# Attention's query products held still in TensorE, with x brought to its partitions by DMAs

## The chip, the cores and the metric

The kernel runs on one core of one Trainium2 chip. The metric is device time in microseconds of one execution; the median of three runs of the kernel before is 496.31 us (496.24 to 496.53). All data is float32.

## The reference

Two blocks follow each other. The first is attention with a polynomial feature map, for 4 batches, 4 heads, 1,088 tokens and head dimension 32. The second is a sum of four two-layer experts over the 4,352 tokens, weighted by gates. Cut to what matters:

```python
def phi(x):                       # 8 x 8 = 64 features of a token
    a = np.einsum('rd,bhsd->bhsr', S1, x)
    b = np.einsum('rd,bhsd->bhsr', S2, x)
    return np.einsum('bhsi,bhsj->bhsij', a, b).reshape(*x.shape[:-1], 64)
q_p, k_p = phi(q), phi(k)
kv = np.einsum('bhsf,bhsd->bhfd', k_p, v)
z = np.sum(k_p, axis=2)
num = np.einsum('bhsf,bhfd->bhsd', q_p, kv)
den = np.einsum('bhsf,bhf->bhs', q_p, z)[..., None] + 1e-06
attn = num / den
x = attn.transpose(0, 2, 1, 3).reshape(4352, 128)      # (token, head x dim)
p = domain_probs / (domain_probs.sum(-1, keepdims=True) + 1e-09)
for e in range(4):
    out += p[:, e:e + 1] * (np.maximum(x @ w1[e], 0) @ w2[e])    # 128 -> 1024 -> 128
```

## The kernel before

The order of all work is written out by hand. A batch's tokens are cut into units (`UNITS`: 128, 480, 480 in batch 0, then 384, 352, 352), for which attention is computed, and all tokens into eleven chunks (`CHUNKS`: 128, 480, 480, five of 512, 320, 256, 128), for which the experts are computed. A chunk has 16 steps, one for each pair of 128-wide blocks of the hidden layer of an expert. The main loop at the end of the program (from line 766) runs over all steps of all chunks; `first` (L573) of a step computes h = x @ w1 and the rectified values and their sums, and `second` (L623), two steps later (`LA`), multiplies them with w2. In the chunks between the first and the last, the second product uses sums of blocks of weights (seven products of 64 x 64 blocks for eight). TensorE works in two halves of 64 output columns each; `on_side` (L184) sends matmuls to the halves in turn, `both` (L190) one to each, and all of them carry the line L188.

Attention is cut into pieces (`front`, L547): a batch's keys are 17 pieces, a unit's queries 19. `work()`, called twice in each step, executes as many pieces as a credit allows. The credit grows by `rate`, so that a chunk's pieces are done 4 pieces before the chunk begins (`needed[c] + 4`); where they are not, they are executed ahead of the chunk's first step. A piece's instructions stand in its engine's order just where it is executed, so an engine does a piece between the instructions of two steps.

For a unit of n tokens, `queries` (L452) turns q in 32 x 32 blocks (`query_turn`, L403), projects it with S1 and S2 on TensorE (`f<-qT,sq`), and makes the feature products `qp` on VectorE (L412; two tiles of 128 features, two heads each). Then `attend` (L419) multiplies: the keys' sums kv, and their divisors z repeated 32 times, both laid out by `key_divide` (L370) in blocks for two heads (`kvz`), stand still in TensorE, and the n columns of `qp` move. The results `den` and `num` have (head, dim) on the partitions and tokens along the free dimension. VectorE turns den, takes reciprocals of one value of 32, turns them back (`rb`) and multiplies num into `xT` (L446). This is the layout that `first` reads as its moving operand: x with its 128 features on the partitions.

The first unit, and the keys of batch 0, are done in `start` (L497) before any chunk. All DMAs are issued on the sync engine's queue (SPq), in program order[...]. They are the loads of k, v and q of a batch (`load_batch`), of the weights, of a chunk's gates, broadcast to 128 partitions (`load_gate`, L299; two buffers), and the stores of a chunk's output (L694, L653).

`weight_sums` on GpSimd is held back until `behind` (L788), a copy of one column of x of unit (0, 128).

Of the kernel before, what the change touches and what calls it, by code (L numbers as in the profile page):

```python
# [23 lines left out]
def kernel(  # L24
# [25 lines left out]
    P = 128  # L50
# [7 lines left out]
    NT = 9  # L58
    FB = F // P
    NQ = E * FB // 2  # L60
    QW = 480
    CW = 512
    GE = 160
    LA = 2
    UNITS = [[P, 480, 480]] + [[384, 352, 352]] * 3

    CHUNKS = [P, 480, 480] + [512] * 5 + [320, 256, P]
    NC = len(CHUNKS)
    START = [sum(CHUNKS[:m]) for m in range(NC)]
    assert all(sum(u) == S for u in UNITS) and sum(CHUNKS) == B * S  # L70
# [12 lines left out]
    def psum(pool, tag):  # L83
        return pool.tile([P, 512], F32, tag=tag, name=tag)
# [27 lines left out]
    def load_batch(b):  # L112
        load_rows(k, b, "kn")
        vn[b] = load_v(b)
        load_rows(q, b, "qn")
# [29 lines left out]
    e_sum = cpool.tile([P, 2, 3], F32, name="e_sum")  # L145
    for i, t in enumerate((0, (B - 1) * S + G - 4)):
        nc.sync.dma_start(
            ends[:, i, :], bass.AP(domain_probs.tensor, domain_probs.offset + t * E, [[E, 4], [G * E, 32], [1, E]])
        )
    load_rows(q, 0, "qn", slice(P, S))  # L150
    for e in range(E):
# [20 lines left out]
    def keep_warm(n):  # L172

        for _ in range(n):
            wp = psum(ps_h, "h")
            nc.tensor.matmul(wp[:, :], warm[:, 0:P], warm[:, :], start=True, stop=True)  # L176

    keep_warm(11)


    turn = [0]
# [123 lines left out]


    FG = ((0, 4), (4, 4), (8, 1))
    fss, kps, kvzs = {}, {}, {}

    def key_turn(b, r):  # L310
        if r < 2:
# [58 lines left out]
    def key_divide(b, kv):  # L370
# [8 lines left out]
            )  # L379
        kvzs[b] = kvz  # L380

    def keys(b):
        for r in range(3):
            key_turn(b, r)
            yield
        for gi, (pool, tag) in enumerate(((ps_f, "f"), (ps_n, "den"), (ps_n, "num"))):
            key_project(b, gi, psum(pool, tag))
            yield
        for _ in value_copy(b):
            pass  # L390
        for t0, n in ((0, 4), (4, 5)):
            for p in range(2):
                for x in range(2):
                    key_product(b, t0, n, p, x, nc.vector)
                    yield
        kv = psum(ps_f, "f")
        for p in range(2):
            key_sum(b, p, kv)
            yield
        key_divide(b, kv)  # L400
        yield

    def query_turn(b, c, n):  # L403
        qT = apool.tile([P, QW], F32, tag="qT", name="qT")
        nc.vector.transpose(qT[:, 0:n], qn[b][:, c : c + n])
        return qT

    def query_tiles():
# [7 lines left out]
            op=ALU.mult,  # L416
        )

    def attend(b, c, n, qp):  # L419
# [12 lines left out]
        yield  # L432
        dT = apool.tile([P, QW], F32, tag="dT", name="dT")
# [7 lines left out]
        rb = apool.tile([P, QW], F32, tag="rb", name="rb")  # L441
# [4 lines left out]
        nc.vector.tensor_tensor(  # L446
            out=xT[:, S * b + c : S * b + c + n], in0=nd[1][:, 0:n], in1=rb[:, 0:n], op=ALU.mult
        )
        have[0] += n
        yield  # L450

# [45 lines left out]
    def start():  # L497


        b, n = 0, UNITS[0][0]  # L500
        kf = []
        for r in range(3):
            key_turn(b, r)
        qT = query_turn(b, 0, n)
        for gi in range(3):
            kf.append(psum(ps_h, "h"))
        value = value_copy(b)
        key_project(b, 0, kf[0])
        next(value)
        key_project(b, 1, kf[1])  # L510
        key_project(b, 2, kf[2])
        for _ in value:
            pass
        fq = [psum(ps_o, "o0"), psum(ps_o, "o1"), psum(ps_n, "num")]
        for i in range(3):
            for j in range(2):
                both(fq[i][:, 0:n], sr[:, i, j, :], qT[:, 0:n], start=(j == 0), stop=(j == 1))
        qb = apool.tile([P, QW], F32, tag="qb", name="qb")
        nc.scalar.copy(qb[:, 0:n], fq[0][:, 0:n])
        for x in range(2):  # L520
# [12 lines left out]
        qp = query_tiles()  # L533
        for x in range(2):
            for p in range(2):
                query_product(qp, p, x, n, fq[1 + x], qb)
        key_divide(b, kv)
        first = attend(b, 0, n, qp)
        next(first)
        keep_warm(4)  # L540
        for _ in first:
            pass
        for h in range(H):
            nc.gpsimd.tensor_copy(_ap(sq, 32 * h, 32, 32 * h, [[R2, 2], [1, R2]]), _ap(s_T, 0, 32, 0, [[D, 2], [1, R2]]))
        gate_sums()

    def front():  # L547
        for b in range(B):
            if b:
                yield from keys(b)  # L550
                if b + 1 < B:
                    load_batch(b + 1)
            c = 0
            for n in UNITS[b]:
                if b or c:
                    yield from queries(b, c, n)
                c += n


# [63 lines left out]
    def second(i):  # L623
# [3 lines left out]
        if plain(m):  # L627

            if f == 0:
                acc[m] = psum(ps_o, f"o{e % 2}")  # L630
            for j in range(2):
                for _ in range(2):
                    on_side(
                        lambda s: acc[m][half[s], 0:DM],
                        lambda s: hd[:, n * j + HP * s : n * j + HP * s + HP],
                        lambda s: w2_sb[:, e, 2 * f + j, :],
                        start=(f == j == 0),
                        stop=(f == NP - 1 and j == 1),
                    )
            if f == NP - 1:  # L640
                p_e = ends[:, 1 if m else 0, e : e + 1]
                if e == 0:
                    total[m] = mpool.tile([P, P], F32, tag="end", name="end")
                    nc.vector.tensor_scalar(
                        out=total[m][:, :], in0=acc[m][:, 0:DM], scalar1=p_e, scalar2=None, op0=ALU.mult
                    )
                else:
                    nc.vector.scalar_tensor_tensor(  # L648
                        out=total[m][:, :], in0=acc[m][:, 0:DM], scalar=p_e, in1=total[m][:, :], op0=ALU.mult, op1=ALU.add
                    )  # L650
                if e == E - 1:
                    t = (START[m] // S) * S + START[m] % S // 32
                    nc.sync.dma_start(  # L653
                        bass.AP(out.tensor, out.offset + t * DM, [[DM, 4], [G * DM, 32], [1, DM]]), total.pop(m)[:, :]
                    )
            return
        if f == 0:
# [109 lines left out]
    for i in range(len(steps) + LA):  # L767
        if i < len(steps):
# [2 lines left out]
                piece()  # L771

            gone = START[m] + CHUNKS[m] * kq / NQ
            rate = CHUNKS[m] / NQ * max([0] + [(needed[c] + 4 - done[0]) / (START[c] - gone) for c in range(m + 1, NC)])

            def work():

# [7 lines left out]
            if i > NQ - 4:  # L785
                if i == NQ - 3:

                    nc.gpsimd.tensor_copy(behind[:, :], xT[:, CHUNKS[0] + CHUNKS[1] - 1 : CHUNKS[0] + CHUNKS[1]])  # L788
                next(to_sum, None)
            if i == 2:  # L790
                gate_quotients()
            elif i == 5:
                store_gates()
                load_gate(1)
                load_gate(2)
                load_batch(1)
            if m > 1 and kq == LA + 3 and m + 2 < NC:
                load_gate(m + 1)
        if i >= LA:
# [35 lines left out]
```

## Time and profile before

| what | value |
|---|---|
| median of three runs | 496.31 us |
| the profiled execution | 495.9 us |
| its span, first to last instruction | 494.1 us |
| granted TensorE clock, mean | 0.999 |
| DMA traffic | 22.36 MB, mean 45 GB/s |

The profiled execution is 1.8 us longer than its span. Busy times of engines are unions of their instructions' times. [...]two matmuls, one in each half, run side by side; so the distance between the starts of groups, and not the duration of one, tells what they cost. In the trace, each float32 matmul of the program stands as two records. Lines of the timeline merge instructions of one kind: start, length, engine, line, operation, output and inputs, count.

The costliest groups of the page, for scale:

```profile
L188 PE MATMUL h<-xT,w_sb 128*64 128x512 f32 (+4 forms) x1408 | 298.3, 495 | 0.4 <-PE h L176 0.4
L584 DVE SCALAR_TENSOR_TENSOR hid<-h,hid 128x256 f32<-128x256 f32 (+6 forms) x432 | 203.7, 472 | 146.9 <-ACT hid L609 138.7
L609 ACT ACTIVATE hid<-h 128x512 f32<-128x512 f32 (+3 forms) x288 | 158.3, 550 | 200.3 <-PE h L188 167.1
```

### The profile page before, as it was taken

The numbers are of one execution on the slowest core, as the hardware profiler recorded it, in microseconds if no ns is written. First come the engines' busy times: TensorE is split into PE (matmuls) and PEld (weight loads), VectorE is DVE, ScalarE is ACT, GpSimd is POOL, SyncE is SP. The second block draws the span as 40 slices with busy tenths as digits, with TensorE's granted clock in tenths as the row PEclk, the third lists the DMA queues.
The fourth block names the chain that finished last, engine by engine and source line by source line (L and its number), as shares of the span: only waits on it lengthen the run. The fifth ranks groups of instructions, "written<-read, shape, count | busy, mean of one in ns | idle before, by whom it ended". The sixth has DMA issues, their size and how long they took to land.

```text
span 494.1 us, 11020 instructions
## 1 busy us (share of the span) xinstructions
PE 487.7 (99%) x4435; PEld 373.7 (76%) x4435; DVE 323.2 (65%) x751; ACT 244.2 (49%) x487; POOL 227.2 (46%) x260
## 2 busy tenths in 40 slices
PE   8999999999999999999999999999999999999996
PEld 5887877777777777777777777777777777778996
DVE  6759666777677576758566647468656657765642
ACT  3344464545454634545445554445445445566751
POOL 6051464435445354425455445335455446555570
PEclk9999999999999999999999999999999999999999
DMA  7981030021002320021002100021001100110000
GB/s 215 277 294 54 2 90 3 1 87 21 0 2 87 85 73 0 1 87 23 0 2 86 21 1 1 2 86 22 2 1 54 22 1 1 44 23 2 15 3 17
DMA packets 29618, 22.36 MB, mean 45 GB/s; under 512 B 19968, under 2 KB 26752, under 8 KB 29184
## 3 DMA queue, kind: packets, MB, share of 16 engines
q1 hardware_dynamic: 29552, 21.66, 15.2%
q8 instruction: 35, 0.57, 0.5%
q14 instruction: 15, 0.12, 0.1%
q10 hardware_dynamic: 16, 0.00, 0.0%
HBM read 19.35 MB, written 2.31 MB: 44 GB/s over the span
## 4 chain that ended last, share of the span: by engine, by line
PE 98%; DVE 1%; DMA 0%; POOL 0%; issue 0%; DVEq 0%
PE h L188 50%; PE o L188 40%; PE f L188 4%; PE den L188 2%; PE num L188 2%; DMA s_raw<-in_S_dram 0%; PE h L176 0%; POOL sr L241 0%; POOL sp L236 0%; DVE end L648 0%; DVE s_e L200 0%; DVE kvz L374 0%; DVE s_f L200 0%; DVE s_T L228 0%; DVE s_hl L227 0%
## 5 line engine op out<-in xcount | busy, mean ns | idle before, releaser
L584 DVE SCALAR_TENSOR_TENSOR hid<-h,hid 128x256 f32<-128x256 f32 (+6 forms) x432 | 203.7, 472 | 146.9 <-ACT hid L609 138.7
L188 PE MATMUL h<-xT,w_sb 128*64 128x512 f32 (+4 forms) x1408 | 298.3, 495 | 0.4 <-PE h L176 0.4
L609 ACT ACTIVATE hid<-h 128x512 f32<-128x512 f32 (+3 forms) x288 | 158.3, 550 | 200.3 <-PE h L188 167.1
L188 PE MATMUL o<-hid,w2s 128*64 128x256 f32 (+3 forms) x1152 | 222.0, 355 | 0.0
L188 PEld LDWEIGHTS h<-xT,w_sb 128*64 128x64 f32 x1408 | 151.2, 137 | 48.8 <-PE h L176 0.9
L188 PE MATMUL o<-hid,w_sb 128*64 128x256 f32 (+3 forms) x864 | 185.5, 355 | 0.0
L188 PEld LDWEIGHTS o<-hid,w2s 128*64 128x64 f32 x1152 | 131.7, 137 | 29.1
L724 POOL TENSOR_TENSOR ev<-yz,sh 64x256 f32<-64x256 f32 (+3 forms) x72 | 48.5, 673 | 159.7 <-ACT sh L727 157.0
L188 PEld LDWEIGHTS o<-hid,w_sb 128*64 128x64 f32 x864 | 102.0, 137 | 20.7
L712 POOL TENSOR_TENSOR yz<-ev 128x512 f32<-128x512 f32 (+3 forms) x36 | 41.9, 1164 | 69.0 <-ACT ev L715 68.8
L724 POOL TENSOR_TENSOR ct<-ev 128x512 f32<-128x512 f32 (+3 forms) x36 | 42.6, 1183 | 2.8
L724 POOL TENSOR_TENSOR ct<-ct,gate 128x512 f32<-128x512 f32 (+3 forms) x27 | 32.0, 1186 | 2.1
L724 POOL TENSOR_TENSOR total<-total,ct 128x512 f32<-128x512 f32 (+3 forms) x27 | 31.9, 1180 | 2.1
L412 DVE TENSOR_TENSOR qp<-qa,qb 64x352 f32<-64x352 f32 (+2 forms) x44 | 29.1, 661 | 1.1
L714 ACT COPY ev<-o 128x512 f32<-128x512 f32 (+3 forms) x36 | 19.3, 537 | 10.1 <-PE o L188 9.6
L188 PE MATMUL o<-w_sb,hid 128*64 128x128 f32 x256 | 22.4, 273 | 0.0
L715 ACT COPY ev<-o 128x512 f32<-128x512 f32 (+3 forms) x36 | 19.4, 538 | 2.5
L188 PEld LDWEIGHTS o<-w_sb,hid 128*64 128x64 f32 x256 | 19.0, 137 | 1.5 <-issue 0.2
L601 ACT ACTIVATE hid<-h 128x256 f32<-128x256 f32 x24 | 9.2, 383 | 21.4 <-PE h L188 20.9
L351 DVE TENSOR_TENSOR kp<-fs 128x256 f32<-128x256 f32 (+1 forms) x24 | 16.2, 682 | 0.0
L727 ACT COPY sh<-yz 64x256 f32<-64x256 f32 (+3 forms) x36 | 13.7, 379 | 1.6 <-POOL yz L712 0.8
L728 ACT COPY sh<-yz 64x256 f32<-64x256 f32 (+3 forms) x36 | 13.7, 379 | 0.9
(102 smaller groups left out, 244.0 us busy)
## 6 DMA issues: line engine op xcount, KB each, us to landing
w_sb<-in_moe_w_dram SPq DMA_DIRECT2D x8, 512.0 KB, 7.3
gate<-gates SPq DMA_DIRECT2D x3, 1024.0 KB, 4.4
kn<-in_k_dram SPq DMA_DIRECT2D x4, 544.0 KB, 4.4
vn<-in_v_dram SPq DMA_DIRECT2D x16, 128.0 KB, 4.1
gate<-gates SPq DMA_DIRECT2D x2, 960.0 KB
qn<-in_q_dram SPq DMA_DIRECT2D x3, 544.0 KB, 3.8
gate<-gates SPq DMA_DIRECT2D x1, 896.0 KB
out_dram<-ob SPq DMA_DIRECT2D x12, 64.0 KB, 2.0
```

The costliest lines, as they stand in the source:

```text
L188: nc.tensor.matmul(out(s), weights(s), moving(s), **flags)
L351: eng.tensor_tensor(out=_ap(kps[b], 0, P, 256 * t0 + P * p + 64 * x, [[256, n], [32, 2], [R, 4], [1, R]]), in0=_ap(src, 0, P, off + 4 * x, ...
L412: nc.vector.tensor_tensor(out=qp[p][64 * x : 64 * x + 64, 0:n], in0=qa[64 * p : 64 * p + 64, 0:n], in1=qb[64 * p : 64 * p + 64, 0:n], op=A ...
L584: nc.vector.scalar_tensor_tensor(out=out, in0=src, scalar=0.0, in1=in1, op0=ALU.max, op1=ALU.subtract)
L601: nc.scalar.activation(hd[:, 0 : 2 * n], hp[:, 0 : 2 * n], ACTF.Relu)
L609: nc.scalar.activation(hd[:, n * j : n * j + n], hp[:, 0:n], ACTF.Relu)
L712: add = lambda out, in0, in1, op=ALU.add: nc.gpsimd.tensor_tensor(out=out, in0=in0, in1=in1, op=op)
L714: nc.scalar.copy(_ap(ev, 0, P, 0, [[2 * w, 2], [1, w]]), _ap(a0, 0, P, 0, two))
L715: nc.scalar.copy(_ap(ev, 0, P, w, [[2 * w, 2], [1, w]]), _ap(a1, 0, P, 0, two))
L724: add = lambda out, in0, in1, op=ALU.add: nc.gpsimd.tensor_tensor(out=out, in0=in0, in1=in1, op=op)
L727: nc.scalar.copy(sh[HP:P, 0:w], yz[0:HP, 0, 0:w])
L728: nc.scalar.copy(sh[0:HP, 0:w], yz[HP:P, 1, 0:w])
```

## The change

In all units but the first, `attend` has its operands changed about: 64 tokens of the query products stand still, and the keys' sums with the sums for the divisors move, 33 columns for each of two heads (`key_blocks`, which takes the place of `key_divide` for batches 1 to 3). The result has tokens on the partitions and, along the free dimension, for each head 32 numerators and a divisor. VectorE takes reciprocals of the divisors, multiplies (`xs`), and turns 32 x 32 blocks (`y`). Tokens and features are then on the right axes, but the 32-partition groups are those of the tokens and not of the heads; sixteen DMAs, one for each of four groups and four heads, bring them to their places in `xT`. `query_turn` permutes tokens so that this works. The first unit keeps the old way (`attend_first`), writing its columns in another order, and `ends` and the last store follow that order.

With it, units and chunks get sizes that are multiples of 64 where needed, pieces are to be done 6 pieces ahead and not 4, a warming matmul is left out at the start, the loads of gate 2 and of batch 1 are issued after the DMAs of unit (0, 128), and `behind` reads `y`.

```diff
-    QW = 480
+    QW = 512
-    UNITS = [[P, 480, 480]] + [[384, 352, 352]] * 3
-    CHUNKS = [P, 480, 480] + [512] * 5 + [320, 256, P]
+    UNITS = [[P, 448, 512]] + [[384, 384, 320]] * 2 + [[384, 320, 384]]
+    CHUNKS = [P, 448, 512] + [512] * 5 + [320, 256, P]
...
-    keep_warm(11)
+    keep_warm(10)
...
+    def key_blocks(b, kv):
+        kvx[b] = apool.tile([P, 2, 2 * (D + 1)], F32, tag="kvx", bufs=2, name="kvx")
+        nc.vector.tensor_tensor(
+            out=_ap(kvx[b], 0, P, 0, [[2 * (D + 1), 2], [D + 1, 2], [1, D + 1]]),
+            in0=_ap(kv, 0, P, 0, [[256, 2], [D + 1, 2], [1, D + 1]]),
+            in1=_ap(own2, 0, P, 0, [[0, 2], [1, 2], [0, D + 1]]),
+            op=ALU.mult,
+        )
...
-        key_divide(b, kv)
-        yield
+        key_blocks(b, kv)
+        yield
+    def unit_parts(b, c, n):
+        return [(0, n - P), (n - P, P)] if b == B - 1 and c + n == S else [(0, n)]
+    def blocks(m):
+        return (m // HP + 1) // 2, m // P
...
     def attend(b, c, n, qp):
         nd = [psum(ps_n, "den"), psum(ps_n, "num")]
+        W = H * (D + 1)
+        tiles = 0
+        laid = []
+        for c0, m in unit_parts(b, c, n):
+            T = blocks(m)
+            for t in range(T[0]):
+                for p in range(2):
+                    for _ in range(2):
+                        at = c0 + P * t + (HP * turn[0] if t < T[turn[0]] else 0)
+                        i, k = divmod(tiles + t, 3)
+                        on_side(
+                            lambda s: nd[i][half[s], W * k + W // 2 * p : W * k + W // 2 * (p + 1)],
+                            lambda s: qp[p][:, at : at + HP],
+                            lambda s: kvx[b][:, p, :],
+                            start=True,
+                            stop=True,
+                        )
+            laid.append((c0, T, tiles))
+            tiles += T[0]
+        yield
...
+        y = apool.tile([P, QW], F32, tag="y", name="y")
+        turned[b, c] = y
+        for c0, T, t0 in laid:
+            nc.vector.transpose(
+                _ap(y, 0, P, P * t0, [[32, T[0]], [32 * T[0], H], [1, 32]]),
+                _ap(xs, 0, P, P * t0, [[P, T[0]], [D, H], [1, D]]),
+            )
+            for a in range(4):
+                s = a // 2
+                at = S * b + c + c0 + 2 * s * 32 * T[0] + a % 2 * 32 * T[s]
+                for h in range(H):
+                    nc.sync.dma_start(
+                        xT[32 * h : 32 * h + 32, at : at + 32 * T[s]],
+                        _ap(y, 32 * a, 32, 32 * (t0 * H + h * T[0]), [[1, 32 * T[s]]]),
+                    )
...
         key_divide(b, kv)
-        first = attend(b, 0, n, qp)
+        first = attend_first(b, 0, n, qp)
...
+        key_blocks(b, kv)
...
+                if b == 0 and c == P:
+                    load_gate(2)
+                    load_batch(1)
...
-            rate = CHUNKS[m] / NQ * max([0] + [(needed[c] + 4 - done[0]) / (START[c] - gone) for c in range(m + 1, NC)])
+            rate = CHUNKS[m] / NQ * max([0] + [(needed[c] + 6 - done[0]) / (START[c] - gone) for c in range(m + 1, NC)])
...
-                    nc.gpsimd.tensor_copy(behind[:, :], xT[:, CHUNKS[0] + CHUNKS[1] - 1 : CHUNKS[0] + CHUNKS[1]])
+                    nc.gpsimd.tensor_copy(behind[:, :], turned[0, P][:, 0:1])
...
                 load_gate(1)
-                load_gate(2)
-                load_batch(1)
```

More of the change, by code (lines that the diff above doesn't have):

```diff
@@ L147 @@
         nc.sync.dma_start(
-            ends[:, i, :], bass.AP(domain_probs.tensor, domain_probs.offset + t * E, [[E, 4], [G * E, 32], [1, E]])
+            ends[:, i, :], bass.AP(domain_probs.tensor, domain_probs.offset + t * E, [[G * E, 32], [1, 4 * E]])
         )
@@ L307 @@
     FG = ((0, 4), (4, 4), (8, 1))
-    fss, kps, kvzs = {}, {}, {}
+    fss, kps, kvzs, kvx = {}, {}, {}, {}
     def key_turn(b, r):
@@ L399, in keys @@
             yield
-        key_divide(b, kv)
+        key_blocks(b, kv)
         yield
+    def unit_parts(b, c, n):
+        return [(0, n - P), (n - P, P)] if b == B - 1 and c + n == S else [(0, n)]
+    def blocks(m):
+        return (m // HP + 1) // 2, m // P
     def query_turn(b, c, n):
         qT = apool.tile([P, QW], F32, tag="qT", name="qT")
-        nc.vector.transpose(qT[:, 0:n], qn[b][:, c : c + n])
+        for c0, m in unit_parts(b, c, n):
+            src = c + c0
+            if b == c == 0:
+                todo = [([[1, m]], [[1, m]], 0, 0)]
+            elif c0:
+                todo = [([[32, 4], [1, 32]], [[1, 4], [4, 32]], 0, 0)]
+            else:
+                T = blocks(m)
+                if T[0] == T[1]:
+                    todo = [([[32 * T[0], 4], [32, T[0]], [1, 32]], [[32, 4], [P, T[0]], [1, 32]], 0, 0)]
+                else:
+                    todo = [
+                        ([[32 * T[s], 2], [32, T[s]], [1, 32]], [[32, 2], [P, T[s]], [1, 32]], 64 * T[0] * s, HP * s)
+                        for s in range(2)
+                    ]
+            for i, o, ci, co in todo:
+                nc.vector.transpose(_ap(qT, 0, P, c0 + co, o), _ap(qn[b], 0, P, src + ci, i))
         return qT
@@ L417, in query_product, with attend_first @@
         )
-    def attend(b, c, n, qp):
+    def attend_first(b, c, n, qp):
         nd = [psum(ps_n, "den"), psum(ps_n, "num")]
@@ L432, in attend @@
         yield
-        dT = apool.tile([P, QW], F32, tag="dT", name="dT")
+        dT = apool.tile([P, P], F32, tag="dT", name="dT")
         nc.vector.transpose(dT[:, 0:n], nd[0][:, 0:n])
@@ L440, in attend @@
         nc.vector.reciprocal(rc[:, 0 : n // 32], rc[:, 0 : n // 32])
-        rb = apool.tile([P, QW], F32, tag="rb", name="rb")
+        rb = apool.tile([P, P], F32, tag="rb", name="rb")
         nc.vector.transpose(
@@ L446, in attend @@
         nc.vector.tensor_tensor(
-            out=xT[:, S * b + c : S * b + c + n], in0=nd[1][:, 0:n], in1=rb[:, 0:n], op=ALU.mult
-        )
+            out=_ap(xT, 0, P, 0, [[1, 4], [4, 32]]),
+            in0=nd[1][:, 0:n].rearrange("p (g j) -> p g j", j=32),
+            in1=rb[:, 0:n].rearrange("p (g j) -> p g j", j=32),
+            op=ALU.mult,
+        )
+        have[0] += n
+        yield
+    turned = {}
+    def attend(b, c, n, qp):
+        nd = [psum(ps_n, "den"), psum(ps_n, "num")]
+        W = H * (D + 1)
+        tiles = 0
+        laid = []
+        for c0, m in unit_parts(b, c, n):
+            T = blocks(m)
+            for t in range(T[0]):
[13 more added lines that the diff above has]
+        yield
+        banks = [(i, 3 * i, min(tiles, 3 * i + 3)) for i in range((tiles + 2) // 3)]
+        rc = apool.tile([P, QW // 32], F32, tag="rc", name="rc")
+        for i, t0, t1 in banks:
+            nc.vector.tensor_scalar(
+                out=rc[:, H * t0 : H * t1],
+                in0=_ap(nd[i], 0, P, D, [[D + 1, H * (t1 - t0)]]),
+                scalar1=1e-6, scalar2=1.0, op0=ALU.add, op1=ALU.mult,
+            )
+        nc.vector.reciprocal(rc[:, 0 : H * tiles], rc[:, 0 : H * tiles])
+        yield
+        xs = apool.tile([P, QW], F32, tag="qa", name="xs")
+        for i, t0, t1 in banks:
+            nc.vector.tensor_tensor(
+                out=_ap(xs, 0, P, P * t0, [[D, H * (t1 - t0)], [1, D]]),
+                in0=_ap(nd[i], 0, P, 0, [[D + 1, H * (t1 - t0)], [1, D]]),
+                in1=_ap(rc, 0, P, H * t0, [[1, H * (t1 - t0)], [0, D]]),
+                op=ALU.mult,
+            )
+        yield
+        y = apool.tile([P, QW], F32, tag="y", name="y")
[4 more added lines that the diff above has]
+                _ap(xs, 0, P, P * t0, [[P, T[0]], [D, H], [1, D]]),
+            )
+            for a in range(4):
[5 more added lines that the diff above has]
+                        _ap(y, 32 * a, 32, 32 * (t0 * H + h * T[0]), [[1, 32 * T[s]]]),
+                    )
@@ L653, in second @@
                     nc.sync.dma_start(
-                        bass.AP(out.tensor, out.offset + t * DM, [[DM, 4], [G * DM, 32], [1, DM]]), total.pop(m)[:, :]
+                        bass.AP(out.tensor, out.offset + t * DM, [[G * DM, 32], [1, 4 * DM]]), total.pop(m)[:, :]
                     )
```

## Prediction

> **What bounds the kernel now.** I read the page first, then the waits of TensorE, the groups by form, and last the timeline of the first chunk and the sync queue's own rows. From the page, the busy row and the lines of the chain of waits:
>
> ```profile
> PE 487.7 (99%) x4435; PEld 373.7 (76%) x4435; DVE 323.2 (65%) x751; ACT 244.2 (49%) x487; POOL 227.2 (46%) x260
> PE 98%; DVE 1%; DMA 0%; POOL 0%; issue 0%; DVEq 0%
> ```
>
> TensorE is busy for 487.7 of 494.1 us and is 98% of the chain. In the answer on waits of TensorE there are four rows, of 1.2, 0.5, 0.4 and 0.3 us, all in the first 14 us. So from the first chunk to the last TensorE never waits: whatever is taken from it shortens the run, and whatever makes it wait lengthens it. VectorE at 65% is hidden.
>
> What a moved column costs is read from the timeline, around one unit's divisors (den) and numerators (num), and from the sums of keys, whose moving side is short:
>
> ```profile
> 9.27 2.30 PE L188 MATMUL f<-vx,kp 128*64 128x66 f32 x72
> ...
> 99.34 1.04 PE L188 MATMUL den<-qp,kvz 128*64 128x384 f32 x4
> 99.98 1.04 PE L188 MATMUL num<-qp,kvz 128*64 128x384 f32 x4
> ```
>
> Each matmul of the program stands as two records (four den matmul records for two in the code). The first num starts 0.64 us after the first den, so four records of 384 columns take 0.64 us: 0.417 ns a column. The 72 records of 66 columns start within 2.30 - 0.22 = 2.08 us: 29.3 ns each, where 66 columns at 0.417 would be 27.5. A later batch has 29 in 1.10 us, which is 31.4. I take 30.5 ns for a short record, between 29.3 and 31.4.
>
> The end of chunk 0 is where the first x by the new way is wanted. From the timeline:
>
> ```profile
> 21.90 1.34 DVE L412 TENSOR_TENSOR qp<-qa,qb 64x480 f32<-64x480 f32 x2
> 23.22 1.10 PE L188 MATMUL den<-qp,kvz 128*64 128x480 f32 x4
> 24.00 0.81 SPq L299 DMA_DIRECT2D gate<-gates  x2
> 24.02 1.10 PE L188 MATMUL num<-qp,kvz 128*64 128x480 f32 x4
> 26.35 0.66 DVE L446 TENSOR_TENSOR xT<-num,rb 128x480 f32<-128x480 f32 x1
> 30.44 0.57 PE L188 MATMUL h<-xT,w_sb 128*64 128x480 f32 x1
> ```
>
> VectorE writes x of unit (0, 128) at 27.0 us, and chunk 1 needs it at 30.44: a margin of 3.4 us, with no DMA between. The new way puts 16 DMAs of the sync queue into that margin. What those cost, from the rows of the stores and from the timeline of that queue:
>
> ```profile
> L694 SPq DMA_DIRECT2D out_dram<-ob x44: 315/464/1819, 110.2 to 486.3; - x44
> DMA to landing us min/median/max: 1.5/1.8/2.0
> ...
> 19.46 1.77 SPq L281 DMA_DIRECT2D gates<-pt  x4
> ```
>
> One issue takes about 0.44 us of the queue when others follow (four gates in 1.77 us; medians 0.43 to 0.46 over the loads), 0.34 when alone. A store lands 1.5 us after its issue began where it is small (8 and 16 KB).
>
> [...]at the start ten warming matmuls stand 0.43 us apart, half rate for 512 columns, then full rate.[...]
>
> **The change part by part.**
>
> (1) TensorE in attend, eleven units, 4,352 - 128 = 4,224 tokens. Removed: 8 records a token-column (4 den, 4 num): 33,792 columns x 0.417 = 14.1 us. Added: a tile of 128 tokens takes 4 matmuls, 8 records, of 66 columns. The units have 4 + 4 tiles in batch 0 and 3 in each of the nine others (320 tokens take 3, the last 384 are 2 + 1): 35 tiles, 280 records x 30.5 = 8.5 us (8.2 to 8.8). Gain 5.5 us (5.3 to 5.9), all of it on the bound engine. The other TensorE work has the same columns: chunks 448 + 512 for 480 + 480, and the query projections cover the same tokens.
>
> (2) VectorE. Per unit two transposes, a reciprocal of 11 to 15 and a multiplication give way to one or two short scalings, the reciprocal, one or two multiplications and one transpose: some 2.1 us (0.54+0.29+0.23+0.55+0.51) become about 1.7. Key_divide's two operations become one. TensorE waits for none of this today, so I cost it at nothing. In the first 15 us kvx (0.28, as kvz) and a split qT (+0.1) come before the query projection; qT ended at 14.58 and the projection began at 15.43, so 0.85 us cover 0.4. One warming matmul fewer: the next one waited for transposed keys and sr in any case.
>
> (3) The wait at chunk 1. In the order of the changed kernel the den matmuls of unit (0, 128) stand at the same step, after the eleventh h of chunk 0. VectorE's steps up to the last qp are 448 wide instead of 480, about 0.035 us less in each of nine, so qp is ready near 22.9; TensorE gets there at 23.22 - 0.05 = 23.17. 32 records x 30.5 = 1.0 us: den and num are complete at 24.3. Then rc of num 0.2, reciprocal 0.25, xs 0.55 + 0.27, y (512 elements, as ob) 0.70: y at 26.3. The sync queue is free: gate(1) was issued at 24.0 to 24.5, and gate(2) and the next batch stand behind now. 16 issues begin 0.44 us apart: the last at 26.33 + 15 x 0.44 = 32.9, landed at 34.45 (1.5). The first h of chunk 1 waits for all 16. TensorE would have been there at 30.44 - 0.6 (attend 1.6 to 1.0) - 0.05 = 29.8. Wait: 4.65 us. [...]h of chunk 1 holds the two last second-products of chunk 0 behind it, and nothing fills the gap. Bounds: issue 0.40 to 0.49, landing 1.3 to 1.9: 3.9 to 5.8 us.[...]
>
> (4) Later chunks. In the new order the last needed y stands as far ahead of its chunk's first h as this. Chunk 3 needs the first 8 copies of unit (1, 384), made in step 13 of chunk 2: VectorE gets to y about 4.2 us into the step, 6.0 us before the chunk; 7 x 0.44 + 1.6 = 4.7. Chunk 5 needs 4 copies, with more time. Chunk 7 needs all 16 of unit (3, 0), step 12 of chunk 6: 11 against 8.3. Chunk 9: y in step 8 of chunk 8, eight stores of 3.8 us ahead of it in the queue, still 4 us to spare. Chunks 2, 4, 6 and 8 have over 20. I take nothing here, and 0 to 2 us for the range. Margin of 6 pieces for 4 is what buys this.
>
> (5) Loads moved behind the copies (gate(2), batch 1): issued near 33.5 to 37.5 instead of 24.4 to 31.4; keys of batch 1 were first turned well after (their TensorE work at 58.9). Nothing. `ends` and the last store have another order of rows and the same count of rows. Nothing.
>
> Sum: -5.5 + 4.65 = -0.9 us on the profiled execution's 495.9, so 495.0; the median of the runs is 496.31, 0.4 above it, and gives 495.4.
>
> **Rivals.**
>
> A, slower: [...]at this kernel's start nine matmuls at 0.43 instead of 0.21 lost 1.9. Then 495.4 + 2.4 = 497.8 (497.1 to 498.8).[...]
>
> B, clearly faster: the copies are plain (32 rows, one run each) and issue at the 0.34 of a lone gate load, landing in 1.2. Wait 26.33 + 5.1 + 1.2 - 29.8 = 2.8, total 493.6. For: gate loads have 0.34 in the median. Against: those are alone or in pairs; every row of followed issues shows 0.43 or more.
>
> C, slower: copies within SBUF cost more than any row here, 0.6 to issue and 2.5 to land. Chunk 1 waits 8.0, chunk 3 0.8, chunk 7 0.6: 500.2. Against: the small loads of vn (16 KB) have 0.43 and 2.4 in a busy queue, the stores 1.5.
>
> **How the numbers follow.** Forecast 495.4 (its own 494.4 to 496.3) has 0.45, A 0.27, B 0.20, C 0.08. 0.2% is about what a measurement can tell: under 495.3 is faster, over 497.3 slower. Faster: B and 0.20 of the forecast, 0.40. Slower: C, 0.22 of A, 0.01: 0.31. Within: 0.29. 493.5 to 498.4 leaves out C and the far ends of A and B, near 0.19.
>
> **What would show it.** Den and num rows of 66 columns with 280 records and about 8.5 us start to start (1); one wait of TensorE on a DMA of xT, 4 to 5.5 us long, at the first h of chunk 1 near 30 us, and none elsewhere (3, 4); copies 0.44 us apart on the sync queue; a granted clock that stays at full in the slice after the gap (against A). It is wrong if TensorE waits at chunks 3 or 7, if the records stand over 35 ns apart, or if the copies start well before or after 26.3 us.

## The result, and the profile after

| | before | after |
|---|---|---|
| median, us | 496.27 (496.11 to 496.53, four runs) | 504.91 (503.79 to 505.85, four runs) |
| ratio to before, 95% interval | | 1.0173 (1.0151 to 1.0194) |
| the profiled execution, us | 495.9 | 505.85 |
| its span, us | 494.1 | 502.8 |
| granted TensorE clock, mean | 0.999 | 0.988 |

The change makes the kernel 8.6 us slower; the forecast was 0.9 us faster, and its range ended at 498.4. From the page of the kernel after, the busy row, the clock row and the chain:

```profile
PE 485.9 (97%) x4626; PEld 361.6 (72%) x4626; DVE 316.0 (63%) x748; ACT 242.8 (48%) x487; POOL 226.9 (45%) x260
...
PEclk9987999999999999999999999999999999999999
...
PE 67%; SPq 2%; DVE 1%; issue 0%; DMA 0%; ACT 0%
```

TensorE is busy for 1.8 us less than before although the span is 8.7 us longer. The sync queue (SPq) has come into the chain, and the fourth slice, 37.7 to 50.3 us, shows a clock of 0.7. What TensorE waited for, in the answer on its waits (total, times, longest):

```profile
PE h L188 <- DMA xT<-y: 9.6, 2, 8.0
PE h L176 <- DVE s_hl L212: 1.2, 1, 1.2
PE h L188 <- DVE qf L568: 0.8, 1, 0.8
...
PE h L188 <- ACT sh L837: 0.3, 1, 0.3
```

Before, no wait of TensorE lay after the start. Where the new ones stand, and what follows the longest, is in TensorE's timeline (start, length, group, count, and in brackets the idle time ahead and what ended it):

```profile
29.75 0.64 PE L188 MATMUL o<-w_sb,hid 128*64 128x128 f32 x8
38.41 3.25 PE L188 MATMUL h<-xT,w_sb 128*64 128x448 f32 x8 [8.02 <-DMA xT<-y]
41.42 1.09 PE L188 MATMUL o<-w_sb,hid 128*64 128x128 f32 x8
42.27 2.54 PE L188 MATMUL h<-xT,w_sb 128*64 128x448 f32 x8
44.63 0.62 PE L188 MATMUL o<-w_sb,hid 128*64 128x128 f32 x8
45.07 1.68 PE L188 MATMUL h<-xT,w_sb 128*64 128x448 f32 x8
46.58 0.35 PE L188 MATMUL o<-hid,w_sb 128*64 128x224 f32 x1
...
145.07 1.94 PE L188 MATMUL h<-xT,w_sb 128*64 128x512 f32 x8 [0.30 <-ACT sh L837]
...
367.92 1.94 PE L188 MATMUL h<-xT,w_sb 128*64 128x512 f32 x8 [0.84 <-DVE qf L568]
...
457.07 1.08 PE L188 MATMUL h<-xT,w_sb 128*64 128x256 f32 x8 [1.62 <-DMA xT<-y]
```

The four rows in brackets are the first h of chunks 1, 3, 7 and 9. Those of 145 and 367 us name another releaser than the copies. ScalarE's sh had ended at 144.78 us and VectorE's qf at 367.82. By the rows of the copies these were late too: chunk 7's sixteen are issued from 356.2 to 365.6 us and land 1.7 us later, the last at 367.3, when TensorE had stood since 367.08; and e2 below, which has both operations and no copies, has neither wait.

The clock after the long wait is in the view of busy time by stretch (stretch, its length, busy time and count for each engine, granted clock, DMA share and GB/s):

```profile
30.00:35.00 5.00, 0.39 (x8) 0.14 (x3) 0.59 (x1) 0.38 (x1) 3.31 (x5) 0.88 0.09 23
35.00:40.00 5.00, 1.59 (x6) 0.66 (x8) 0.00 (x0) 0.00 (x0) 0.00 (x0) 0.50 0.43 166
40.00:45.00 5.00, 5.00 (x30) 2.61 (x28) 1.73 (x4) 1.78 (x4) 0.00 (x0) 0.60 1.06 302
45.00:50.00 5.00, 5.00 (x44) 2.98 (x41) 4.57 (x13) 2.24 (x5) 0.00 (x0) 1.00 0.33 104
```

TensorE is idle from 30.39 us. A mean of 0.88 in the first stretch means half clock for its last 1.2 us, so the fall is at 33.8; 0.60 in the third means full clock for its last microsecond, so it ends at 44.0, 5.6 us after work was there again. And the cause of the wait, in the rows of the copies (count, ns min/median/max, first and last start) between 26 and 38 us, and their landing over the whole kernel:

```profile
L550 SPq DMA_DIRECT2D xT<-y x16: 582/589/617, 26.8 to 36.3; - x16
...
DMA to landing us min/median/max: 1.6/1.8/3.8
```

Sixteen issues take 9.5 us from the first to the last start, 0.63 us apart and not 0.44.

### The profile page after: what moved, and what is told of

It is laid out like the page before. It is cut to its first block, busy times and chain, and to the rows that moved or that the text cites. A ratio compares the mean times of both kernels' runs of the same rounds, so it can differ in the third digit from the quotient of the medians.

```text
span 502.8 us, 11675 instructions
## 1 busy us (share of the span) xinstructions
PE 485.9 (97%) x4626; PEld 361.6 (72%) x4626; DVE 316.0 (63%) x748; ACT 242.8 (48%) x487; POOL 226.9 (45%) x260
## 4 chain that ended last, share of the span: by engine, by line
PE 67%; SPq 2%; DVE 1%; issue 0%; DMA 0%; ACT 0%
PE h L188 35%; PE o L188 29%; PE f L188 2%; SPq L550 2%; PE den L188 1%; DVE hid L693 0%; DMA xT<-y 0%; ACT hid L718 0%; PE num L188 0%; ACT sh L837 0%; DVE qf L568 0%; DVE end L757 0%
## 5 line engine op out<-in xcount | busy, mean ns | idle before, releaser
L188 PE MATMUL o<-hid,w2s 128*64 128x256 f32 (+3 forms) x1152 | 227.0, 355 | 0.0
L188 PEld LDWEIGHTS h<-xT,w_sb 128*64 128x64 f32 x1408 | 142.7, 138 | 65.2 <-issue 22.2
L188 PE MATMUL o<-hid,w_sb 128*64 128x256 f32 (+3 forms) x864 | 181.0, 355 | 0.0
L188 PEld LDWEIGHTS o<-hid,w2s 128*64 128x64 f32 x1152 | 134.3, 137 | 23.5
L448 DVE TENSOR_TENSOR qp<-qa,qb 64x384 f32<-64x384 f32 (+3 forms) x44 | 29.9, 679 | 1.1
L188 PE MATMUL o<-w_sb,hid 128*64 128x128 f32 x256 | 20.1, 277 | 0.0
L188 PEld LDWEIGHTS o<-w_sb,hid 128*64 128x64 f32 x256 | 16.1, 140 | 2.3 <-issue 2.1
L836 ACT COPY sh<-yz 64x256 f32<-64x256 f32 (+3 forms) x36 | 13.7, 379 | 1.8 <-POOL yz L821 0.9
L188 PEld LDWEIGHTS den<-kvx,qp 128*64 128x64 f32 x264 | 12.0, 137 | 3.0 <-issue 1.5
L351 DVE TENSOR_TENSOR kp<-fs 128x256 f32<-128x256 f32 (+1 forms) x24 | 14.1, 591 | 0.0
```

Of the source, the lines that this page charges most:

```text
L188: nc.tensor.matmul(out(s), weights(s), moving(s), **flags)
L351: eng.tensor_tensor(out=_ap(kps[b], 0, P, 256 * t0 + P * p + 64 * x, [[256, n], [32, 2], [R, 4], [1, R]]), in0=_ap(src, 0, P, off + 4 * x, ...
L448: nc.vector.tensor_tensor(out=qp[p][64 * x : 64 * x + 64, 0:n], in0=qa[64 * p : 64 * p + 64, 0:n], in1=qb[64 * p : 64 * p + 64, 0:n], op=A ...
L836: nc.scalar.copy(sh[HP:P, 0:w], yz[0:HP, 0, 0:w])
```

## The experiments

Two theories stood at first. T1: the copies come too late at chunk 1, by their own issue in one queue, and the idle time then halves the clock; both together outweigh what TensorE gained. T2: the loss is spread over the kernel, through the new sizes, the order of pieces, or the traffic of 192 copies beside the loads and stores.

**e1: the unit with the short margin keeps the old attention.** Unit (0, 128) gets x from `attend_first`, with no copies; the others are as changed. The edit's main line (with it, that unit's tokens keep the old order, and `behind` reads x again):

```diff
-        yield from attend(b, c, n, qp)
+        yield from (attend_first if b == 0 and c == P else attend)(b, c, n, qp)
```

> Unit (0, 128) alone keeps the old attend, written straight to x; all other units have the new one with its copies. If the loss is the wait for 16 copies at chunk 1 (8.0 us) and the half clock after it (2.8), both go and 0.65 of gain goes with them: 504.9 - 10.8 + 0.65 = 494.8, with TensorE's only DMA wait the 1.6 us at chunk 9. If the copies cost all along, or the short matmuls don't gain, it stays above 497.

Measured: 494.3 us (493.85 to 495.15), ratio 0.9965 (0.9954 to 0.9976): 10.6 us less than the changed kernel, from one of the eleven changed units, and near the 494.8 expected. Waits on x at three chunks are left where one was expected. What is left of waits on x, in the answer on TensorE's waits:

```profile
PE h L188 <- DVE qf L568: 1.9, 2, 1.0
PE h L188 <- DMA xT<-y: 1.4, 1, 1.4
```

They are at the first h of chunks 3, 7 and 9 again, 3.3 us in all. So the loss at chunk 1 is more than the whole loss, and beside it there are three small ones.

**e2: no copies at all.** VectorE turns `xs` straight into x; the sixteen DMAs of each unit are gone, and the blocks stay on the partitions of their tokens.

```diff
...
-                    nc.sync.dma_start(
-                        xT[32 * h : 32 * h + 32, at : at + 32 * T[s]],
-                        _ap(y, 32 * a, 32, 32 * (t0 * H + h * T[0]), [[1, 32 * T[s]]]),
-                    )
+            nc.vector.transpose(xT[:, S * b + c + c0 : S * b + c + c0 + m], _ap(xs, 0, P, P * t0, [[1, m]]))
```

> All 192 copies are left out: VectorE turns the blocks straight into x, so x has its values in wrong places and the output is not the reference's. If the copies are the whole loss: 504.9 - 8.0 - 2.8 - 1.6 = 492.5 or a little less, no DMA wait on TensorE; that is also what the change is worth with transport for nothing (3.8 under before, where my prediction had 5.5). If the new operands or the new sizes cost TensorE time, 496 or more.

Measured: 489.44 us (489.32 to 489.91), ratio 0.9865 (0.985 to 0.988), and no wait of TensorE after the start. That is 3.1 us below the 492.5 expected, which had counted only the two waits named as DMA and the half clock. This is what the change would be worth if the transport cost nothing: 6.65 us against the 496.09 of before, measured beside it. It also serves as a ruler for the changed kernel, since all else is the same. Starts of the first h of chunks in the two timelines, and the end of the span:

| us | c1 | c2 | c3 | c6 | c7 | c8 | c9 | c10 | end |
|---|---|---|---|---|---|---|---|---|---|
| after | 38.41 | 89.84 | 145.07 | 311.11 | 367.92 | 420.93 | 457.07 | 483.50 | 502.8 |
| e2 | 29.82 | 78.47 | 133.05 | 299.07 | 354.70 | 407.69 | 441.95 | 468.36 | 487.6 |
| added since the start before | 8.59 | 2.78 | 0.65 | 0.02 | 1.18 | 0.02 | 1.88 | 0.02 | 0.1 |

15.2 us in all, in five places: the wait at chunk 1, the half clock after it, and the starts of chunks 3, 7 and 9. (0.37 of the first 8.59 are a later start of the whole: the first h of chunk 0 stands at 14.52 us, and in e2 at 14.15.)

**e5: the sizes alone.** The kernel before with the new units, chunks, 6 pieces ahead for 4, and 10 warming matmuls for 11.

> The kernel before with the new units, chunks, pieces 6 ahead and ten warming matmuls, and nothing else of the change. If sizes are neutral as predicted, 496.3 (495.8 to 496.8). If they cost, 497 to 498, and that explains part of the gain that is missing.

Measured: 495.9 us (495.81 to 496.38), ratio 0.9997 (0.9988 to 1.0006). This is as expected: the sizes do nothing. With e2 this ends T2 but for the traffic of the copies.

**e4: the same copies, to device memory.** The 192 copies are issued as before, but write to a scratch tensor that nobody reads, and x is made as in e2. So queue and DMA engines carry them, and TensorE waits for none of them.

```diff
...
-                        xT[32 * h : 32 * h + 32, at : at + 32 * T[s]],
+                        beside[32 * h : 32 * h + 32, 32 * a * T[0] : 32 * a * T[0] + 32 * T[s]],
```

> The changed kernel with each of the 192 copies writing the same block to a scratch tensor in device memory and not to x; x gets the blocks straight from VectorE, in wrong places, so the output is not the reference's and nothing waits for the copies but the reuse of y. If an issue is dear because both ends lie in SBUF, the 16 issues of a unit take 7.0 to 7.4 us here (0.44 to 0.46 each) and not 10.1. If 32 rows of one run each are dear wherever they go, 10.1 again. The time is 489.4 to 490 if copies cost only by being waited for; 491 to 492 if they also slow the engines in the background (the 2.6 us that the run with unit (0, 128) old lost between chunks 1 and 8 against the run without copies).

Measured: 489.8 us (489.71 to 490.28), ratio 0.9872 (0.9857 to 0.9886), 0.4 us over e2, which the two intervals do not tell apart. The traffic beside the kernel costs next to nothing. The rows of these copies show why the forecast's price was wrong:

```profile
L550 SPq DMA_DIRECT2D beside<-y x192: 302/419/1992, 26.6 to 449.2; - x192
...
DMA to landing us min/median/max: 1.3/1.5/3.6
```

The same rows from the same tile take 0.42 us to issue and 1.5 to land where they go to device memory, and 0.59 and 1.8 where they go to SBUF. In rows of sixteen with no long issue among them the starts are 0.46 us apart here (127.52 to 134.38 us), and 0.63 in the changed kernel. The change of partitions is not the reason: of the sixteen copies at chunk 1 four stay on their 32 partitions, and they take 0.59 to 0.62 us like the others. Why an issue within SBUF takes longer stays open. The forecast had taken the price of stores and loads for that of copies within SBUF.

**e3: the gap kept warm.** 24 matmuls on the warming tile stand ahead of the first h of chunk 1, to hold the clock.

```diff
+            if i == NQ:
+                keep_warm(24)
```

> The changed kernel with 24 warming matmuls (5.1 us at full clock) put ahead of chunk 1's first h, in the gap. If the half clock follows from the gap, the copies still land at 38.4 us, TensorE's clock stays at full and 2.8 us are won: 502.1. If the half clock has another cause, or the clock falls all the same in the 2.9 us left of the gap, 504.9.

Measured: 505.99 us (505.35 to 506.18), ratio 1.0198 (1.0181 to 1.0215). The timeline of TensorE:

```profile
30.03 5.35 PE L176 MATMUL h<-warm 128*128 128x512 bf16 x24
38.63 2.31 PE L188 MATMUL h<-xT,w_sb 128*64 128x448 f32 x8 [3.25 <-DMA xT<-y]
```

The 24 end 3.25 us before x is there, and in the stretch from 40 to 45 us the clock is 0.69: it falls all the same, from 39.6 to 43.1 us. So this run doesn't tell what the half clock costs; it shows that 3.25 us of idle time can suffice for a fall.

**e8: the gap kept warm to its end.** The same with 36 warming matmuls.

> As the run with 24 warming matmuls in the gap, with 36 (7.7 us): the gap left is 1 us or less. In that run a rest of 3.25 us still had the clock at half from about 39.3 to 43.8. If the gap's length is the cause, the clock is full throughout, chunk 2's first h comes at 87.0 to 87.2 (89.8 in the changed kernel), and the time is 502.1 to 503. If a wait on a DMA of any length is followed by half clock, 505 again.

Measured: 505.26 us (504.41 to 506.09), ratio 1.0181 (1.0162 to 1.02). TensorE's timeline:

```profile
30.34 7.94 PE L176 MATMUL h<-warm 128*128 128x512 bf16 x36
38.94 1.72 PE L188 MATMUL h<-xT,w_sb 128*64 128x448 f32 x8 [0.65 <-PE h L176]
40.46 0.64 PE L188 MATMUL o<-w_sb,hid 128*64 128x128 f32 x8
40.90 1.70 PE L188 MATMUL h<-xT,w_sb 128*64 128x448 f32 x8
42.40 0.64 PE L188 MATMUL o<-w_sb,hid 128*64 128x128 f32 x8
42.84 1.70 PE L188 MATMUL h<-xT,w_sb 128*64 128x448 f32 x8
44.34 0.35 PE L188 MATMUL o<-hid,w_sb 128*64 128x224 f32 x1
```

The work that took 46.58 - 38.41 = 8.17 us in the changed kernel takes 44.34 - 38.94 = 5.40 here: the half clock cost 2.8 us there, and chunk 2 begins 2.2 us earlier. The whole kernel is no faster, though, and the 505 that it takes is the number expected for a fall after any wait, although the clock held at chunk 1. In this trace the wait at chunk 7 has grown to 1.96 us and that at chunk 9 to 2.24, and the clock falls to half after the latter for 3.4 us. Of its four executions two have a mean clock of 0.997 and take 506.1 us, two have 1.0 and take 504.4.

**e9: both gaps kept warm.** e8, with eight more warming matmuls ahead of chunk 9. It was run to see whether the clock is all that e8 lost again.

> 36 warming matmuls ahead of chunk 1, as in the kernel e8, and eight (1.7 us) ahead of chunk 9, where e8 still stood 2.2 us and went on at half clock. If the half clock is what the gaps cost beside their own length, both falls go: the changed kernel's 504.9 less 2.2 (chunk 1, as measured in e8's stage) and with nothing lost after chunk 9, 502.2 (501.5 to 503.3), clock 1.0 throughout after the start. If the clock is not what made e8 as slow as the changed kernel, it stays at 504.5 to 505.5.

Measured: 504.35 us (503.92 to 504.7), ratio 1.0165 (1.015 to 1.018), a mean clock of 1.0: 0.6 us less than the changed kernel, not the 2.7 expected. So the clock is not all. Chunk 2 begins at 87.31 us, 2.5 earlier, as it should; chunk 8 at 419.49, only 1.4 earlier. In between, from the rows of TensorE's waits and of the copies between 352 and 368 us:

```profile
PE h L188 <- DMA xT<-y: 1.9, 1, 1.9
```

```profile
L550 SPq DMA_DIRECT2D xT<-y x16: 513/588/1682, 353.6 to 364.1; - x16
```

Chunk 7 waits 1.9 us and not 0.8, since one of its sixteen issues took 1.68 us instead of 0.59. The same is in e8 (1.69), where chunk 7 waits 1.96. In the changed kernel the longest of these sixteen was 0.60. The copies themselves begin 2.5 us earlier than in the changed kernel, at 353.6 us for 356.2, so what was won at chunk 1 is not waited away there: the long issue loses it. At chunk 9 one of the sixteen copies that h waits for takes 1.64 us, where in the changed kernel none of them is over 0.60, and the gap ahead of h is 2.3 us with the warming in it, for 1.6.

The long issues have something in common, in the trace's list of DMA packets. The changed kernel's page counts 36 loads on a queue for instructions, 16 KB each:

```profile
q8 instruction: 36, 0.59, 0.5%
```

In the changed kernel eight of the 192 copies take over 0.8 us to issue, and during each of the eight such a load is under way; in e8 it is so for nine of nine, and in e9 for ten of ten. Around chunk 7's copies the loads of the changed kernel begin at 348.4 and 369.0 us, outside them; with the 36 more matmuls of e8 and e9 one begins at 358.9 and at 358.5 us, and the long issue at 358.9 and at 358.6. So these two warmed kernels lost at chunk 7 because their long issue, and with it 1.1 us, fell on copies that TensorE waits for. That the load is what holds the issue is argued from this agreement alone; no run moved the loads by themselves.

**e10: two queues for the critical sixteen.** ScalarE's queue issues the eight copies of the odd heads of unit (0, 128), SP's queue the other eight.

```diff
-                    nc.sync.dma_start(
+                    (nc.scalar if b == 0 and c == P and h % 2 else nc.sync).dma_start(
```

> The changed kernel with the eight copies of odd heads of unit (0, 128) issued by ScalarE's queue and the other eight by SP's. If the time of the issues in one queue is what makes the first h of chunk 1 late (0.63 us each in the changed kernel), each queue is through at 26.8 + 8 x 0.63 = 31.8 and x is there at 33.6 with a landing of 1.8: the wait falls from 8.0 to about 3.2 us (some of it may stand under ScalarE's rectified values of chunk 0, which wait behind its own issues), and with a clock that still falls after such a gap the kernel takes 504.9 - 4.8 = 500.1 (499 to 502.5). If the transfers themselves, and not their issue, set the pace, the interval doubles in each queue and the wait stays near 8 us: 504.5 to 505.5.

Measured: 499.57 us (498.08 to 501.25), ratio 1.0059 (1.0041 to 1.0076), as the first case has it. The two queues, and TensorE's waits:

```profile
26.46 6.06 SPq L550 DMA_DIRECT2D xT<-y  x8
26.46 5.11 ACTq L550 DMA_DIRECT2D xT<-y  x8
```

```profile
PE o L188 <- ACT hid L710: 3.3, 1, 3.3
```

The two queues issue side by side: ScalarE's eight are 0.64 us apart as before, SP's 0.78 in the mean, with a wait of 0.7 us for an earlier DMA among them (in the answer on the sync queue's waits). Sixteen transfers begin within 5.5 us and not 9.5, so it is the issue in one queue, and not the transfers, that set the pace. But TensorE now stands 3.3 us earlier on, at an o of chunk 0: ScalarE's rectified values stand in its order behind its own eight issues, which end at 31.57 us, and begin at 31.67. The clock falls to half after this gap too, and again after the wait at chunk 9, of 2.2 us.

**e6: by device memory.** Each unit's y is stored to a scratch tensor in four DMAs, one for each group of 32 partitions and all heads, and comes back in one load of 128 partitions: 5 issues for 16.

```diff
...
-                for h in range(H):
-                    nc.sync.dma_start(
-                        xT[32 * h : 32 * h + 32, at : at + 32 * T[s]],
-                        _ap(y, 32 * a, 32, 32 * (t0 * H + h * T[0]), [[1, 32 * T[s]]]),
-                    )
+                nc.sync.dma_start(
+                    xd[:, at : at + 32 * T[s]].rearrange("(h r) w -> r h w", r=32),
+                    _ap(y, 32 * a, 32, 32 * t0 * H, [[32 * T[0], H], [1, 32 * T[s]]]),
+                )
+            nc.sync.dma_start(xT[:, S * b + c + c0 : S * b + c + c0 + m], xd[:, :])
```

> Blocks go through device memory: four stores and one load for a unit in place of sixteen copies. At chunk 1: y at 26.5, four stores issued by 28.4, landed by 30.6, one load 2.4 more: 33.0, a wait of 3 us for 8. If the number of issues is what costs, 489.4 + 3 = 492.4 with the clock held, 494.2 if a gap of 3 us still drops it; no wait at chunk 9. If the transport's latency costs, two in a row make it worse than the copies at every chunk where these waited: over 500.

Measured: 492.88 us (492.07 to 493.67), ratio 0.9927 (0.991 to 0.9945). The sync queue and TensorE's first h of chunk 1, in the timeline:

```profile
26.55 1.75 SPq L551 DMA_DIRECT2D xd<-y  x4
...
29.70 0.34 SPq L555 DMA_DIRECT2D xT<-xd  x1
...
32.32 2.66 PE L188 MATMUL h<-xT,w_sb 128*64 128x448 f32 x8 [2.15 <-DMA xT<-xd]
```

Though data goes out and in, with a wait for the stores between, x is there 6.1 us earlier, and the waits at chunks 3, 7 and 9 are gone. The clock falls even after this gap, by the view by stretch:

```profile
32.00:33.00 1.00, 0.68 (x4) 0.40 (x6) 0.00 (x0) 0.00 (x0) 1.00 (x2) 0.98 0.98 401
33.00:34.00 1.00, 1.00 (x5) 0.34 (x3) 0.00 (x0) 0.41 (x1) 0.16 (x1) 0.50 1.07 418
...
36.00:37.00 1.00, 1.00 (x6) 0.39 (x4) 0.61 (x2) 0.00 (x0) 0.00 (x0) 0.81 1.15 247
```

Its four executions tell what that costs: two have a mean clock of 1.0 and take 492.07 and 492.24 us, two have 0.997 and take 493.52 and 493.67. In the same program the clock falls in one execution and not in another, for 1.4 us. The time lies between the 492.4 expected with the clock held and the 494.2 with a fall.

**e7: both.** Unit (0, 128) keeps the old attention as in e1, and the other ten units go by device memory as in e6.

> Through device memory for all units but (0, 128), which keeps the old attend: no unit is wanted at once any more. 489.4 + 0.65 = 490.1, up to 491 with some wait on VectorE; no DMA wait on TensorE. If what the run with unit (0, 128) old lost between chunks 1 and 8 is not from the copies, 492.7.

Measured: 491.37 us (490.72 to 491.51), ratio 0.9899 (0.9884 to 0.9913), clock 1.0. Of TensorE's waits for x one of 0.5 us is left, at the first h of chunk 3 (put down to VectorE's hid, as other waits for x were put down to other engines above). 490.1 to 491 were expected. It beats both kernels, by 5.0 us the one before and by 13.5 the changed one.

## Why the prediction was wrong

**Step (1), TensorE's gain: right, a little small.** After shows 24 records of 66 columns between the starts of den and num, from TensorE's timeline:

```profile
23.59 0.90 PE L188 MATMUL den<-kvx,qp 128*64 128x66 f32 x24
24.29 0.43 PE L188 MATMUL num<-kvx,qp 128*64 128x66 f32 x8
```

0.70 / 24 = 29.2 ns each for the 30.5 taken; 280 of them make 8.2 us, and the gain 5.9 for 5.5. e2 puts the change without its copies at 6.65, with the store of step (5) in it. (The forecast's "29 in 1.10 us" are records of 64 columns; 33 of 66 columns in a later batch of the kernel before take 1.21 us, 30.9 ns each.)

**Step (2), VectorE and the start: right.** y of unit (0, 128) was done at 26.74 us, for the 26.3 forecast. TensorE had ended its last matmul before chunk 1 at 38.41 - 8.02 = 30.39; in unbroken work the next begins 0.2 us before such an end (e2), so it was there at 30.2, for 29.8. Both stand 0.4 us late, as the first h of chunk 0 does (14.52 for 14.10), so the margin was as computed.

**Step (3), the wait at chunk 1: here it failed, by the size of a term.** The sum was the right one, last issue plus landing less TensorE's arrival; "16 issues begin 0.44 us apart" was the term. It was read from stores and gate loads, which have one end in device memory. Copies within SBUF are 0.63 apart: 15 x 0.19 = 2.9 us of the missing 3.4, and the landing of 1.8 for 1.5 gives 0.3 more. What was shown in its place: 16 copies are 9.5 us from the first issue to the last, and TensorE waits 8.0 us. e4 shows the two prices side by side and e10 that the issue in one queue is what counts. The bounds of 0.40 to 0.49 were a spread over rows of the wrong kind; no row of the kernel before had both ends in SBUF, so the bound had to be wider than the rows it was taken from. Rival C named 0.6 and 8.0 us, and was given 0.08.

**Rival A held as alone was part of the same case.** A is half clock after the gap, C the longer wait, and here they are one event: after the 8.02 us the clock was at half until 43.99 us, which cost 2.8 us (e8). A's price of 2.4 and its chance were the author's estimate: the longest of the four waits in the kernel before is 1.2 us, and no trace had shown half clock after idle time. C and A together were in no case: 495.4 + 3.4 + 2.8 is 501.6, and the chances treated them as exclusive.

**Step (4), nothing at later chunks: wrong.** The same issue interval eats those margins: waits of 0.3 us at chunk 3, 0.8 at chunk 7, 1.6 at chunk 9. C had the first two at 0.8 and 0.6. The last was held to have 4 us to spare, and there the interval is not the whole: the first sixteen of the last unit's 32 copies, for which chunk 9 waits, begin at 445.60 us, 9.85 before TensorE is through at 455.45, and 15 x 0.44 + 1.6 = 8.2 would have left 1.6. The eight stores ahead of them in the queue take 4.7 us for the 3.8 counted (3.8 in e2); one of them takes 1.41, and an instruction load is under way then too, from 443.1 us.

**Step (5), order of loads and of the last store: the store was counted at nothing and gained half a microsecond.** The forecast said "the same count of rows"; in the code the last store's 128 rows of device memory, each on its own, have become 32 runs of four rows. From the sync queue's waits, the kernel before and after:

```profile
SPq L830 <- DMA out_dram<-end: 1.9, 1, 1.9
```

```profile
SPq L937 <- DMA out_dram<-end: 1.4, 1, 1.4
```

e5, which has the old store, shows 1.9 too, and every run with the new one 1.2 to 1.5. The loads that were moved behind the copies cost nothing in e2 and e4, and the sizes nothing in e5, as forecast.

**The sum.** On the spans: -5.9 for attend, -0.5 for the store, +8.0 for the wait, +2.8 for the clock, +1.1 for chunks 3 and 7, +1.6 for chunk 9 make +7.1. Measured are 502.8 - 494.1 = +8.7. Of the 1.6 that remain 0.4 are the later start, and most of the rest is what idle times leave out: in e2 the first h of chunks 1, 3, 7 and 9 begins 0.20, 0.34, 0.34 and 0.20 us before the matmul ahead of it has ended by the profile, and a wait loses this overlap as well. That makes 1.1, and 0.1 is open. The profiled execution was the slowest of its four: its clock was 0.988, that of the fastest (503.79) 0.993.

## What to carry to other kernels

Price a new DMA by rows of the same kind, at both ends; where there is none, let the bound reach half as far again as the nearest row (here 0.63 us for 0.44), and multiply it by the number that one queue issues in a row ahead of the waiting work. A chain of small copies on one queue was long through its issues here, so fewer and larger DMAs won even by a detour through device memory: 5 issues had x in place 6.1 us before the 16 copies. And where a TensorE-bound kernel may stand for some 2 us or more, add the half clock behind the gap to the same case, with a chance (six gaps of 2.15 to 8.02 us here were followed by it, one of 2.54 was not; the last section has what it went with), and look at the clock of every execution and not of one.

## What the runs showed that was not expected

- A copy from SBUF to SBUF took 0.59 us to issue on the sync queue and 1.8 to land; the same rows to device memory 0.42 and 1.5. ScalarE's queue issued at the same pace (0.60). Single issues took up to 2.0 us. Over the seven kernels with these copies (e4 among them), 61 of the 62 issues of over 0.8 us on the sync queue overlap a 16 KB load of instructions, and of the other 1,258 only 47 do.
- In these traces the fall of the clock to half after a gap went with where the gap lies, and not with its length alone. Within each trace the instants at which the clock changes are whole multiples of 3.413 us apart: in the changed kernel it falls at 33.75, is full again at 43.99 and falls after the last matmuls at 501.38, which makes 10.24 us, 3 times, and 457.39 us, 134 times. So each trace can be cut into windows of 3.41 us by one of its changes. What TensorE was busy in a window, from the view by stretch, and what the clock did at its end:

| run, gap at | gap, us | window | TensorE busy of 3.41 us | clock at its end |
|---|---|---|---|---|
| after, chunk 1 | 8.02 | 30.34 to 33.75 | 0.04 | falls |
| e10, end of chunk 0 | 3.35 | 29.46 to 32.88 | 0.77 | falls |
| e3, chunk 1 | 3.25 | 36.23 to 39.64 | 1.00 | falls |
| e8, chunk 9 | 2.24 | 453.83 to 457.24 | 1.17 | falls |
| e6, chunk 1 | 2.15 | 29.55 to 32.96 | 1.26 | falls |
| e10, chunk 9 | 2.16 | 449.30 to 452.72 | 1.26 | falls |
| e5, end of the last matmuls | | 488.70 to 492.11 | 1.40 | stays |
| e9, chunk 7 | 1.94 | 362.99 to 366.40 | 1.55 | stays |
| e8, chunk 7 | 1.96 | 365.08 to 368.49 | 1.70 | stays |
| after, chunk 9 | 1.62 | 453.59 to 457.01 | 1.86 | stays |
| e3, chunk 9 | 2.54 | 452.65 to 456.07 | 2.25 | stays |
| e3, chunk 9 | the same | 456.07 to 459.48 | 2.04 | stays |

In these traces a window with at most 1.26 us of work (37%) is followed by half clock, and one with 1.40 us (41%) or more is not. e3's gap of 2.54 us had no fall: a window's end cuts it in two, and 2.25 and 2.04 us of work are left in the two windows. Half clock lasted one window after each of the shorter gaps, beginning 0.6 to 1.1 us after work was there again, and three windows after the longest: the first of these had no work, the second, with 2.17 us of it (64%), did not bring the full clock back, and the third, wholly busy, did. A wholly idle window was not needed: the limit in these traces lies between 59% and 63% idle, with the ends of matmuls as the profile models them. The clock of e6 fell in two of four executions; where the windows lay in the other three than the profiled one was not shown.
